# A DeltaNet and SwiGLU kernel: the first two chunks' inverse in 16x16 blocks, weights converted by an integer add, the plain FFN in whole passes

## The chip, the core and the metric

The kernel runs on one core of a Trainium2 chip. The core has five engines with a queue each: TensorE (PE) multiplies matrices into PSUM, VectorE (DVE), ScalarE (ACT) and GpSimd (POOL) work element by element, and SyncE (SP) mostly issues DMAs, as ACT's queue can too. An engine takes its instructions strictly in order and waits on semaphores for the others. The metric is device time in microseconds; less is better.

## The reference

```
k_n = k / (|k| + 1e-6)                        # B=4, H=8, S=768, D=48
for t in range(S):
    y[t] = q[t] @ state                       # per batch and head, state 48 x 48
    state += beta[t] * k_n[t] (v[t] - state^T k_n[t])^T
x = y as (B*S, H*D) = (3072, 384)
xn = x / sqrt(mean(x^2) + 1e-6) * g
out = (silu(xn @ w_gate) * (xn @ w_val)) @ w_out      # 384 -> 1536 -> 384
```

q, k, v and beta are fp32; the weights and g come as float64, which the kernel reads as pairs of 32-bit words and converts to fp32 itself.

## The kernel before

The sequence is cut into 12 chunks of 64 tokens. In a chunk the recurrence is a triangular system: with A the strictly lower part of beta * k_n k_n^T (64x64 for each of 32 pairs of batch and head), u = (1 + A)^-1 beta (v - k_n state), y = q state + mask(q k_n^T) u, and the state gains k_n^T u. `prep(c)` forms the scores and inverts (`scores`, L538), `recur(c)` makes u, y and the state (products with the state L849, with the inverse L895, with u L909 and L946), and y is transposed for the FFN (`xtr`, L1017) and scaled by g into `xf`, or `xp1` in chunk 1 (L1021).

The inverse is taken in 32x32 blocks. Scores are written to DRAM (`dkk`) and read back so that each of 128 partitions holds one 32x32 block (`at_`); DVE scales the block by beta (L654), takes a first pair of columns (L679 to L689) and then 15 steps of two instructions, a product (L701) and a sum of three (L707). The result goes through DRAM (`dx`) into `mt`, `x2bd` and `m1bd`, and PE makes the block below the diagonal in two merges (L783, L807); chunks 0 and 1 turn one block on PE as well (L759). Chunk 0 works on unscaled keys at first and divides by the norms afterwards (L607, L623 to L629).

The FFN of chunks 0 and 1 is plain (`ffn_plain`: up-projections L1084, ACT's silu L1091, DVE's product L1092, down-projections L1066); its 12 column blocks run in two halves, chunk 0's first half, chunk 1's first half, then the second halves, with the partial results in `part`. Chunks 2 to 11 use a form of fewer products (`ffn`, L1177, and `down`, L1234) on sums of weights that `factors` (L1140, L1142) and `out_factors` (L1213) make once.

The 18 weight pieces of 128 x 768 values pass three raw buffers. One takes an ACT pass (L465), two DVE passes on bits (L453, L456), one DVE pass that multiplies in the low word (L461), and a sum, by PE for the first three pieces (L478 to L483) and by DVE for the others (L486).

Nothing runs in source order. Each operation is handed to a planner (`Plan`) with an estimated duration, a priority and its dependencies; the planner simulates the engines, searches 60 orders and emits the best. `due(c, lead)` gives the time by which something of chunk c should be ready; `P.lead` puts the recurrence in front of the FFN on PE. Until a planned time of 70 us the planner fills PE's gaps with matmuls of `ident` (`fillers`, L1334), into one bank of PSUM set aside for that. The order is fixed when the kernel is built.

## Time and profile before

| what | us |
|---|---|
| runs | 714.55, 711.37, 714.91 (middle 714.55) |
| span of the profiled execution | 711.6 |
| mean granted clock of TensorE | 0.995 |

The page gives no time of the profiled execution beside its span. A group's row reads: line, engine, operation, output and inputs, shapes, count, busy us, mean ns of one, idle time before it. These rows of the page stand for the stage from chunk 2 on:

```profile
L1187 DVE TENSOR_TENSOR tmp<-tmp,bank 128x512 f32<-128x512 f32 x180 | 122.2, 685 | 88.6 <-PE bank L1177 63.0
L1177 PE MATMUL bank<-xf,w_in 128*128 128x128 f32 x1440 | 182.0, 277 | 0.0
L1177 PE MATMUL bank<-xf,more 128*128 128x128 f32 x960 | 123.9, 277 | 0.0
```

DVE idles 88.6 us in front of its additions there, mostly for PE, while these matmuls of PE wait for nothing. Matmuls are pipelined, so the mean of one (277 ns) is longer than the distance between two; prices of PE's work are taken from how long a row of many lasts.

### The profile page before, as it was taken

The numbers are of one execution on the slowest core, as the hardware profiler recorded it, in microseconds if no ns is written. First come the engines' busy times: TensorE is split into PE (matmuls) and PEld (weight loads), VectorE is DVE, ScalarE is ACT, GpSimd is POOL, SyncE is SP. The second block draws the span as 40 slices with busy tenths as digits, with TensorE's granted clock in tenths as the row PEclk, the third lists the DMA queues.
The fourth block names the chain that finished last, engine by engine and source line by source line (L and its number), as shares of the span: only waits on it lengthen the run. The fifth ranks groups of instructions, "written<-read, shape, count | busy, mean of one in ns | idle before, by whom it ended". The sixth has DMA issues, their size and how long they took to land.

```text
span 711.6 us, 23292 instructions
## 1 busy us (share of the span) xinstructions
PE 698.8 (98%) x10036; PEld 634.8 (89%) x10036; DVE 545.9 (77%) x1139; ACT 317.7 (45%) x755; POOL 135.4 (19%) x140
## 2 busy tenths in 40 slices
PE   8998998999999999999999999999999999999997
PEld 5656777777799999999999999999999998999997
DVE  4899998999648959938959948946969847976473
ACT  5435553334244445546435355345355355234441
POOL 4201203102021232223130405005040304000000
PEclk9999998999999999999999999999999999999999
DMA  7777895431351261271161262154161161040000
GB/s 138 214 156 179 221 247 137 59 62 35 51 103 25 47 111 34 55 125 34 30 114 25 46 120 51 26 99 85 17 113 17 37 99 33 13 65 2 23 1 23
DMA packets 210071, 54.67 MB, mean 77 GB/s; under 512 B 199216, under 2 KB 202288, under 8 KB 209968
## 3 DMA queue, kind: packets, MB, share of 16 engines
q1 hardware_dynamic: 205120, 52.26, 36.8%
q10 hardware_dynamic: 4848, 0.92, 0.8%
q8 instruction: 79, 1.29, 0.7%
q14 instruction: 24, 0.20, 0.1%
HBM read 40.83 MB, written 12.32 MB: 75 GB/s over the span
## 4 chain that ended last, share of the span: by engine, by line
PE 89%; DVE 6%; DMA 2%; POOL 1%; ACT 1%; issue 1%; POOLq 0%; ACTq 0%; DVEq 0%
PE bank L1177 38%; PE bank L1234 20%; PE bank L1084 9%; PE bank L1066 4%; PE bank L849 3%; PE bank L538 3%; PE bank L515 3%; PE bank L909 2%; DVE acc L707 2%; PE bank L895 2%; PE bank L1334 1%; PE bank L1017 1%; DVE acc L701 1%; PE bank L946 1%; PE bank L783 1%; PE bank L807 1%
## 5 line engine op out<-in xcount | busy, mean ns | idle before, releaser
L1187 DVE TENSOR_TENSOR tmp<-tmp,bank 128x512 f32<-128x512 f32 x180 | 122.2, 685 | 88.6 <-PE bank L1177 63.0
L1177 PE MATMUL bank<-xf,w_in 128*128 128x128 f32 x1440 | 182.0, 277 | 0.0
L1177 PEld LDWEIGHTS bank<-xf,w_in 128*128 128x128 f32 x1440 | 170.1, 192 | 2.6 <-issue 1.2
L1177 PE MATMUL bank<-xf,more 128*128 128x128 f32 x960 | 123.9, 277 | 0.0
L1177 PEld LDWEIGHTS bank<-xf,more 128*128 128x128 f32 x960 | 115.1, 192 | 1.5 <-issue 0.4
L1189 ACT COPY tmp<-bank 128x512 f32<-128x512 f32 x120 | 68.7, 584 | 65.4 <-PE bank L1177 57.2
L707 DVE TENSOR_REDUCE acc<-acc 128x30 f32<-128x90 f32 (+4 forms) x180 | 85.0, 472 | 6.2
L1193 ACT ACTIVATE tmp<-tmp 128x256 f32<-128x256 f32 x120 | 49.5, 417 | 74.5 <-DVE tmp L1187 74.0
L701 DVE TENSOR_TENSOR acc<-acc,at 128x60 f32<-128x60 f32 (+4 forms) x180 | 63.1, 351 | 2.6
L1234 PE MATMUL bank<-wo_sb,hf 128*128 128x192 f32 x360 | 63.9, 328 | 0.0
L1194 DVE TENSOR_TENSOR hf<-tmp 128x256 f32<-128x256 f32 x120 | 53.9, 463 | 12.6 <-ACT tmp L1193 11.4
L560 POOL TENSOR_TENSOR knrm<-ksum,half 128x16 f32<-128x16 f32 x12 | 36.5, 3043 | 121.3 <-DVE ksum L559 121.3
L1234 PEld LDWEIGHTS bank<-wo_sb,hf 128*128 128x128 f32 x360 | 58.1, 190 | 0.5 <-DVE hf L1194 0.2
L1334 PE MATMUL bank<-ident 128*128 128x128 f32 (+2 forms) x156 | 45.2, 437 | 1.4 <-POOL ident masks.py:199 1.4
L1334 PEld LDWEIGHTS bank<-ident 128*128 128x128 f32 x156 | 26.3, 197 | 18.9 <-issue 16.4
L654 POOL TENSOR_TENSOR at<-at,beta_b 128x1024 f32<-128x1024 f32 x8 | 18.9, 2364 | 117.0 <-DMA at<-dkk 94.7
L728 POOL COPY acc<-acc 128x128 f32<-128x128 f32 x40 | 16.5, 445 | 129.2 <-DVE acc L707 128.5
L1084 PE MATMUL bank<-xf,w_in 128*128 128x256 f32 x144 | 33.6, 384 | 0.5 <-ACT xf L1021 0.5
L1084 PE MATMUL bank<-xp,w_in 128*128 128x256 f32 x144 | 34.0, 394 | 0.0
L1066 PE MATMUL bank<-wo_sb,hf 128*128 128x384 f32 x96 | 33.6, 490 | 0.0
L1084 PEld LDWEIGHTS bank<-xp,w_in 128*128 128x128 f32 x144 | 28.1, 198 | 4.4
L1084 PEld LDWEIGHTS bank<-xf,w_in 128*128 128x128 f32 x144 | 26.7, 190 | 5.1 <-ACT xf L1021 0.7
(166 smaller groups left out, 1018.8 us busy)
## 6 DMA issues: line engine op xcount, KB each, us to landing
at<-dkk SPq DMA_DIRECT2D x23, 256.0 KB, 4.2
q<-in_q_dram SPq DMA_DIRECT2D x24, 192.0 KB, 3.8
more<-in_moe_w_val_dram SPq DMA_DIRECT2D x6, 768.0 KB, 6.1
more<-in_moe_w_gate_dram SPq DMA_DIRECT2D x6, 768.0 KB, 6.6
more<-in_moe_w_out_dram SPq DMA_DIRECT2D x6, 768.0 KB, 7.3
vt<-in_v_dram SPq DMA_DIRECT2D x24, 192.0 KB, 4.5
out_dram<-tmp SPq DMA_DIRECT2D x48, 96.0 KB, 2.2
k<-in_k_dram SPq DMA_DIRECT2D x23, 192.0 KB, 4.2
```

The costliest lines, as they stand in the source:

```text
L560: P.add("POOL", 2.95, lambda: nc.gpsimd.tensor_tensor(out=knrm[i2], in0=ksum[i2], in1=half, op=ALU.pow), pn, r=[("ksum", i2), "half"], w=[ ...
L701: nc.vector.tensor_tensor(out=acc[:, 1:3, 0:n, j + 2 : W].rearrange("p a i t -> p i a t"), in0=acc[:, old, 0:n, j : j + 2, None].to_broadc ...
L707: nc.vector.tensor_reduce(out=acc[:, new, 0:n, j + 2 : W], in_=acc[:, lo : lo + 3, 0:n, j + 2 : W].rearrange("p a i t -> p i t a"), axis=A ...
L1066: nc.tensor.matmul(po[p].t[:, 0:DM], hf[:, spot(f), 128 * p : 128 * p + 128], wo_sb[:, spot(f)], start=(f == f0), stop=(f == f1 - 1), skip ...
L1084: nc.tensor.matmul(ps.t[:, TOK * side : TOK * side + TOK], w_in[:, side, h_, 3 * t + i_, n : n + 128], x_[:, 2 * t : 2 * t + 2].rearrange( ...
L1177: nc.tensor.matmul(g.t[:, 128 * z : 128 * z + 128], fac[:, side, 128 * f : 128 * f + 128], xf[:, xs], start=(begin and z == 0), stop=False ...
L1187: P.add("DVE", V(512), lambda t=t, g=g: nc.vector.tensor_tensor(out=t, in0=t, in1=g.t, op=ALU.add), -1, r=[g], w=[tk], last=g)
L1189: P.add("ACT", A(512), lambda t=t, g=g: nc.scalar.copy(t, g.t), -1, r=[g], w=[tk], last=g)
L1193: P.add("ACT", A(256), lambda t=t: nc.scalar.activation(out=t[:, 0:256], in_=t[:, 0:256], func=ACTF.Silu), -1, w=[tk])
L1194: P.add("DVE", V(256), lambda t=t, f0=f0, p=p: nc.vector.tensor_tensor(out=hf[:, spot(f0) : spot(f0) + 2, 128 * p : 128 * p + 128], in0=t[ ...
L1234: nc.tensor.matmul(g.t[:, 0:192], a_[:, f], b_[:, f], start=(begin and f == 0), stop=(f == 5), skip_group_check=True)
L1334: nc.tensor.matmul(warm[:, 0 : 128 * w_].rearrange("p (w n) -> p w n", n=128), ident, ident[:, None, :].to_broadcast([128, w_, 128]))
```

## The change

Chunks 0 and 1 get an inverse of their own (`invert`), and nothing of it passes DRAM. From the scores, taken once per half of the heads, DVE multiplies by a coefficient per row (for chunk 0 it holds beta and the norms, `gam`, so that the keys need no scaling there; beta comes as rows that PE transposes, `betas`), folds the diagonal 32x32 blocks together, turns them by a VectorE transpose, picks the 16x16 blocks, runs 7 steps of the same kind as before on 16 columns, and turns back with four transposes. Two merges on PE (n = 0: 16 to 32, n = 1: 32 to 64), each a product with L and one with X for each half, make the full inverse; X is turned from its transpose by DVE before each merge. `recur` uses the transposed inverse directly (`mr0`) for chunks 0 and 1.

A weight piece takes two ACT passes (the high word as before, and the low word scaled by 2^-29 and written as an integer), one DVE shift and one DVE addition of 32-bit integers; PE's sums are gone. All pieces may be issued from 2 us on. The plain FFN of chunk 0 runs whole behind its recurrence, then that of chunk 1; `part` is gone. Fillers end at a planned 40 us and use free banks, no bank is set aside, and some operations carry an `urgent` priority. `due` moves from 64, 90, 160 + 51 (c - 2) to 42, 92, 143 + 51 (c - 2). Operations from chunk 2 on are the same, in a new order.

```diff
+    T0, UNTIL, V0, V1 = 42.0, 40.0, 10.0, 40.0
     def due(c, lead):
-        return (64.0 - min(lead, 64.0)) if c == 0 else (90.0 if c == 1 else 160.0 + PERIOD * (c - 2)) - lead
+        return (T0 - min(lead, T0)) if c == 0 else T0 + 50.0 + PERIOD * (c - 1) - lead
...
-            def s2(u=u):
-                nc.vector.tensor_scalar(out=u, in0=u, scalar1=3, scalar2=None, op0=ALU.logical_shift_left)
-
-            def s4(u=u, cc=cc):
-                nc.vector.tensor_scalar(
-                    out=cc.bitcast(U32), in0=u, scalar1=0xFF800000, scalar2=None, op0=ALU.bitwise_and
-                )
-
-            def s5(low=low, cc=cc, by=2.0**-52):
-                nc.vector.scalar_tensor_tensor(out=cc, in0=low, scalar=by, in1=cc, op0=ALU.mult, op1=ALU.mult)
-
...
+            def shifted(top=top):
+                nc.vector.tensor_scalar(out=top, in0=top, scalar1=3, scalar2=None, op0=ALU.logical_shift_left)
+            def added(dst=dst.bitcast(U32), top=tiled(top), rest=tiled(rest)):
+                nc.vector.tensor_tensor(out=dst, in0=top, in1=rest, op=ALU.add)
+            P.add("ACT", 0.84, lambda high=high, top=cva[a]: nc.scalar.activation(out=top, in_=high.bitcast(FP32), func=ACTF.Prelu, scale=2.0**-112, alpha=2.0**32), pr, r=[("raw", i)], w=cak)
+            P.add("ACT", 0.84, lambda low=low, rest=rest: nc.scalar.activation(out=rest, in_=low, func=ACTF.Copy, scale=2.0**-29), pr, r=[("raw", i)], w=cvk)
+            P.add("DVE", 0.57, shifted, pr, w=cak)
+            done = [("cv", n)]
+            P.add("DVE", 0.97, added, pr, r=cvk + cak, w=done)
...
+        if c == 0:
+            by_p = lambda t, p: t[:, p:16:2]
+            for p in range(2):
+                P.add("POOL", 1.6, lambda p=p: nc.gpsimd.tensor_tensor(out=by_p(knrm[0], p), in0=by_p(ksum[0], p), in1=by_p(half, p), op=ALU.pow), pn, r=[("ksum", 0), "half"], w=[("knrm", 0, p)])
+                def inv(p=p):
+                    nc.vector.tensor_scalar_add(by_p(knrm[0], p), by_p(knrm[0], p), 1e-6)
+                    nc.vector.reciprocal(by_p(krec[0], p), by_p(knrm[0], p))
+                    nc.vector.tensor_tensor(out=by_p(rb, p), in0=by_p(bt0[:, 0], p), in1=by_p(krec[0], p), op=ALU.mult)
+                    nc.vector.scalar_tensor_tensor(out=by_p(gam, p), in0=by_p(rb, p), scalar=-1.0, in1=by_p(krec[0], p), op0=ALU.mult, op1=ALU.mult)
...
+    def invert(c, pr):
+        ktk = [("kt", c % NKQ, hv) for hv in range(2)]
+        coef, ck = ((gam, [("gam", 0), ("gam", 1)]), (nbt, ["nbt"] * 2))[c]
+        L, X, XT = lx[c], xx[c], xxt[c]
+        key = lambda n, p: (n, c, p)
+        xtk = lambda p: [(key("xxt", p), i) for i in range(2)]
+        view = lambda ps, n: ps.t[:, 0 : 8 * n].rearrange("s (y n) -> s y n", n=n)
+        later = lambda lead: pr + lead
+        sp = [Group(), Group()]
+        for p in range(2):
+            def sc(p=p):
+                for u, g in units:
+                    m = kt[c][low(p), u, low(g)]
+                    nc.tensor.matmul(sp[p].t[low(g), 64 * u : 64 * u + 64], m, m)
+            P.rows = 64
+            P.add("PE", 0.53, sc, later(0.1 * p), r=ktk, w=[sp[p]], ps=sp[p], size=64)
+            P.rows = 128
+        for p in range(2):
+            P.add("DVE", 0.72, lambda p=p: nc.vector.tensor_tensor(
+                out=L[:, p], in0=view(sp[p], C), in1=coef[:, p:16:2, None].to_broadcast([128, 8, C]), op=ALU.mult,
+            ), later(1), r=[sp[p], ck[p]], w=[key("lx", p)], last=sp[p])
+            P.add("ACT", A(256), lambda p=p: nc.scalar.mul(lc[:, p], L[:, p, :, 0:W], side32[:, 0:1]), later(1), r=[key("lx", p), "sides"], w=[("lc", p)])
+            P.add("DVE", V(256), lambda p=p: nc.vector.scalar_tensor_tensor(
+                out=lc[:, p], in0=L[:, p, :, W:C], scalar=side32[:, 1:2], in1=lc[:, p], op0=ALU.mult, op1=ALU.add,
+            ), later(1), r=[key("lx", p), "sides"], w=[("lc", p)])
+        lcf = lc.rearrange("s q y n -> s (q y n)")
+        P.add("DVE", 0.66, lambda: nc.vector.transpose(out=turned, in_=lcf.rearrange("s (r j) -> s j r", j=16)), later(1.5), r=[("lc", 0), ("lc", 1)], w=["turned"])
+        def align():
+            nc.vector.tensor_scalar(out=a16, in0=turned[:, :, 0:16], scalar1=odd[:, 0:1], scalar2=None, op0=ALU.mult)
+            nc.vector.scalar_tensor_tensor(out=a16, in0=turned[:, :, 16:32], scalar=odd[:, 1:2], in1=a16, op0=ALU.mult, op1=ALU.add)
+        P.add("DVE", 0.72, align, later(2), r=["turned", "sides"], w=["a16"])
+        def start():
+            e = nc.gpsimd if c else nc.vector
+            e.memset(acc16[:, 0:4:3], 0.0)
+            e.memset(acc16[:, 0:4:3].rearrange("s a c t -> s a (c t)")[:, :, 0:256:17], 1.0)
+        P.add("POOL" if c else "DVE", 0.9 if c else 0.5, start, 0, w=["acc16"])
+        diag = a16.rearrange("s j t -> s (j t)")[:, 1 : 1 + 34 * 7 + 1 : 34]
+        def share():
+            nc.vector.tensor_tensor(out=pair16[:, :, 0:8], in0=a16[:, :, 0:16:2], in1=diag[:, None, :].to_broadcast([128, 16, 8]), op=ALU.mult)
+            nc.vector.tensor_copy(out=acc16[:, 0:4:3].rearrange("s a c t -> s a (c t)")[:, :, 1 : 1 + 34 * 7 + 1 : 34], in_=diag[:, None, :].to_broadcast([128, 2, 8]))
+            nc.vector.tensor_tensor(out=a16[:, :, 1:16:2], in0=a16[:, :, 1:16:2], in1=pair16[:, :, 0:8], op=ALU.add)
+        P.add("DVE", 0.75, share, later(3), w=["a16", "acc16"])
+        for j in range(0, 14, 2):
+            n, m = j + 2, 14 - j
+            def step(j=j, n=n, m=m):
+                old, new, lo = (3, 0, 1) if j % 4 else (0, 3, 0)
+                nc.vector.tensor_tensor(
+                    out=acc16[:, 1:3, 0:n, j + 2 : 16].rearrange("s a c t -> s c a t"),
+                    in0=acc16[:, old, 0:n, j : j + 2, None].to_broadcast([128, n, 2, m]),
+                    in1=a16[:, None, j : j + 2, j + 2 : 16].to_broadcast([128, n, 2, m]),
+                    op=ALU.mult,
+                )
+                nc.vector.tensor_reduce(
+                    out=acc16[:, new, 0:n, j + 2 : 16], in_=acc16[:, lo : lo + 3, 0:n, j + 2 : 16].rearrange("s a c t -> s c t a"), axis=AXL.X, op=ALU.add
+                )
+            P.add("DVE", 0.47 + 0.0052 * n * m, step, later(4), r=["a16"], w=["acc16"])
+        def back():
+            for side in range(2):
+                for f in range(2):
+                    t0 = 2 * side + f
+                    nc.vector.transpose(
+                        out=xc16.rearrange("s q y z t -> s t (q y z)")[:, t0:16:4],
+                        in_=acc16[:, 3 * side, :, t0:16:4].rearrange("s c k -> s k c")[:, :, None, :].to_broadcast([128, 4, 2, 16]),
+                    )
+        P.add("DVE", 1.0, back, later(8), r=["acc16"], w=["xc16"])
+        for p in range(2):
+            P.add("DVE", V(256), lambda p=p: nc.vector.tensor_tensor(
+                out=XT[:, p, :, 0:W].rearrange("s y (z t) -> s y z t", z=2), in0=xc16[:, p],
+                in1=side16[:, None, 0:2, None].to_broadcast([128, 8, 2, 16]), op=ALU.mult,
+            ), later(9), r=["xc16", "sides"], w=[(key("xxt", p), 0)])
+            def place(p=p):
+                for z in range(2):
+                    nc.scalar.mul(XT[:, p, :, W + 16 * z : W + 16 * z + 16], xc16[:, p, :, z], side16[:, 2 + z : 3 + z])
+            P.add("ACT", 0.6, place, later(9), r=["xc16", "sides"], w=[(key("xxt", p), 1)])
+        for n in range(2):
+            s = 16 << n
+            cut = lambda t, s=s: t.rearrange("s y (a two i) -> s y a two i", two=2, i=s)[:, :, :, 1]
+            each = lambda t, s=s: t.rearrange("s y (a i) -> s y a i", i=s)
+            for p in range(2):
+                P.add("DVE", 0.4 if n else 0.66, lambda p=p, e=W if n else C: nc.vector.transpose(out=X[:, p, :, 0:e], in_=XT[:, p, :, 0:e]), later(10 + 5 * n), r=xtk(p), w=[key("xx", p)])
+                P.rows = 64
+                wp, xp_ = Group(), Group()
+                def mw(p=p, wp=wp, s=s):
+                    for u, g in units:
+                        nc.tensor.matmul(
+                            wp.t[low(g), W * u : W * u + W], L[low(g), p, u],
+                            XT[low(g), p, u].rearrange("s (a two i) -> s a two i", two=2, i=s)[:, :, 1],
+                        )
+                P.add("PE", 0.7, mw, later(10 + 5 * n), r=[key("lx", p)] + xtk(p), w=[wp], ps=wp, size=64)
+                if n:
+                    P.add("ACT", A(256), lambda p=p, wp=wp: nc.scalar.mul(wx[:, p], view(wp, W), side32[:, 0:1]), later(11 + 5 * n), r=[wp, "sides"], w=[("wx", p)], last=wp)
+                else:
+                    P.add("DVE", V(256), lambda p=p, wp=wp, each=each: nc.vector.tensor_tensor(
+                        out=each(wx[:, p]), in0=each(view(wp, W)), in1=side16[:, None, 0:4:2, None].to_broadcast([128, 8, 2, 16]), op=ALU.mult,
+                    ), later(11 + 5 * n), r=[wp, "sides"], w=[("wx", p)], last=wp)
+                def mxt(p=p, xp_=xp_):
+                    for u, g in units:
+                        nc.tensor.matmul(xp_.t[low(g), W * u : W * u + W], X[low(g), p, u], wx[low(g), p, u])
+                P.add("PE", 0.7, mxt, later(12 + 5 * n), r=[key("xx", p), ("wx", p)], w=[xp_], ps=xp_, size=64)
+                P.rows = 128
+                P.add("DVE", V(256), lambda p=p, xp_=xp_, cut=cut, each=each: nc.vector.tensor_tensor(
+                    out=cut(XT[:, p]), in0=cut(XT[:, p]), in1=each(view(xp_, W)), op=ALU.add,
+                ), later(13 + 5 * n), r=[xp_], w=xtk(p), last=xp_)
...
+        kkeys, kp = kkeys_(c), [("k2p", c % NK)]
         ktk = [("kt", ikq, hv) for hv in range(2)]
-
+        if c:
+            P.add("POOL", 1.6, lambda: nc.gpsimd.tensor_tensor(
+                out=kd, in0=kd, in1=krec[i2][:, :, None].to_broadcast([128, 16, D]), op=ALU.mult,
+            ), pr if c == 1 else due(c, 125), r=[("krec", i2)], w=kkeys)
+        turn(kn, kt[ikq], ktk, kkeys + kp, pr, c == 0)
+        if c < 2:
+            invert(c, pr)
+            return
         fast = c < 4
...
+        rhs, rhsk = r_, rk
+        if c == 0:
+            P.add("POOL", 1.6, lambda: nc.gpsimd.tensor_tensor(out=vt, in0=vt, in1=rb[:, :, None].to_broadcast([128, 16, D]), op=ALU.mult), 5, r=[("gam", 0), ("gam", 1)], w=vk)
...
+            def mr0(p=p, gu=gu):
+                for bb in range(2):
+                    for y_ in range(4):
+                        for g in range(2):
+                            rows, x_, n = slice(64 * g, 64 * g + 64), 8 * bb + 4 * p + y_, 48 * (4 * bb + y_)
+                            nc.tensor.matmul(gu.t[rows, n : n + 48], xxt[c][rows, x_ % 2, x_ // 2], rhs[rows, x_])
...
-        if c == 1:
-
-            ffn_plain(0, 0, FT // 2, due(0, 0))
-            ffn_plain(1, 0, FT // 2, due(1, 0))
-            ffn_plain(0, FT // 2, FT, due(1, 0) + 23)
-            ffn_plain(1, FT // 2, FT, due(1, 0) + 46)
-            factors(0)
-            factors(1)
-            out_factors()
-        elif c > 1:
+        if c < 2:
+            ffn_plain(c, 0, FT, due(c, 0))
+            if c:
+                factors(0)
+                factors(1)
+                out_factors()
+        else:
             ffn(c, due(c, 0))
...
-        P.run([(0.0, t) for t in banks[:7]] + [(70.0, warm)], filler, 70.0)
+        P.run([(0.0, t) for t in banks], filler, UNTIL)
```

310 lines of the change are left out of this document (146 added, 164 removed).

## The prediction

> **What bounds the kernel now.** I read the page's first part, then a table of windows cut where the work changes, then the timelines of TensorE, VectorE, ScalarE and GpSimd up to 200 us.
>
> ```profile
> span 711.6 us, 23292 instructions
> PE 698.8 (98%) x10036; PEld 634.8 (89%) x10036; DVE 545.9 (77%) x1139; ACT 317.7 (45%) x755; POOL 135.4 (19%) x140
> ```
> ```profile
> 0.00:74.00 74.00, 68.73 (x858) 45.44 (x858) 59.34 (x128) 34.13 (x77) 16.54 (x19) 1.00 0.77 169
> 74.00:124.00 50.00, 47.92 (x832) 38.21 (x833) 46.66 (x81) 23.97 (x52) 8.80 (x5) 0.93 0.83 210
> 124.00:198.00 74.00, 74.00 (x655) 57.47 (x654) 63.77 (x129) 25.91 (x64) 9.43 (x12) 1.00 0.30 51
> 198.00:355.00 157.00, 156.97 (x2591) 152.40 (x2590) 121.33 (x269) 75.87 (x182) 37.64 (x37) 1.00 0.34 63
> ```
> ```profile
> 61.93 1.63 PE L895 MATMUL bank<-vt,mt 64*64 64x48 f32 x64
> 74.01 6.74 PE L1084 MATMUL bank<-xf,w_in 128*128 128x256 f32 x30 [0.46 <-ACT xf L1021]
> 197.93 1.05 PE L1177 MATMUL bank<-xf,more 128*128 128x128 f32 x8
> ```
>
> The columns of the windows are length, then busy time of PE, PEld, DVE, ACT, POOL, then granted clock, DMA share, GB/s. From 198 us on PE has no gap (156.97 of 157): there the end moves only with the amount of matmuls or with the time at which that stage starts. Before 74.01, where the first matmul of the plain FFN stands, PE's 68.73 us are mostly fillers and small products, and DVE works through the 32x32 inverse of chunk 0 and the weights. Between 74 and 198 both engines are nearly full. So the change is worth what it moves 74.01 forward, less what PE then waits before the stage at 198.
>
> **The chain of chunk 0, rebuilt.** Durations are from these rows; the order on each engine is that of the changed kernel as built.
>
> ```profile
> 8.85 0.17 DVE L559 TENSOR_SCALAR ksum<-ksum 128x16 f32<-128x16 f32 x1
> 12.27 0.25 DVE L564 RECIPROCAL krec<-knrm 128x16 f32<-128x16 f32 x1
> 12.64 1.29 DVE L607 SCALAR_TENSOR_TENSOR pt<-bank,krec 128x512 f32<-128x512 f32 x2
> 15.30 0.56 DVE L456 TENSOR_SCALAR more<-more 128x768 uint32<-128x768 uint32 x1
> 15.90 0.96 DVE L461 SCALAR_TENSOR_TENSOR more<-more 128x768 f32<-128x768 uint32 x1
> 45.77 0.96 DVE L486 TENSOR_TENSOR w_in<-more 128x768 f32<-128x768 f32 x1
> 28.26 0.22 DVE L701 TENSOR_TENSOR acc<-acc,at 128x60 f32<-128x60 f32 x1
> 28.81 0.28 DVE L701 TENSOR_TENSOR acc<-acc,at 128x112 f32<-128x112 f32 x1
> 29.50 0.32 DVE L701 TENSOR_TENSOR acc<-acc,at 128x156 f32<-128x156 f32 x1
> 41.27 0.28 DVE L707 TENSOR_REDUCE acc<-acc 128x30 f32<-128x90 f32 x1
> 79.30 0.41 DVE L1092 TENSOR_TENSOR hf<-tmp,bank 128x256 f32<-128x256 f32 x1
> ```
> ```profile
> 16.62 0.39 SPq L367 DMA_DIRECT2D more<-in_moe_w_gate_dram  x1
> 21.09 0.92 ACT L465 ACTIVATE xf<-more 128x768 f32<-128x768 f32 x1 [1.60 <-DMA more<-in_moe_w_gate_dram]
> 64.49 0.33 ACT L971 ACTIVATE yn<-bank 128x192 f32<-128x192 f32 x1 [0.58 <-PE bank L909]
> 64.72 0.19 ACT L971 ACTIVATION_READ_ACCUMULATOR yn<-bank 128x1 f32 x1
> 67.27 0.73 ACT L1004 ACTIVATE yn<-bank,rs 128x192 f32<-128x192 f32 x2
> 73.59 0.88 ACT L1021 ACTIVATE xf<-bank,g_sb 128x128 f32<-128x128 f32 x3 [0.63 <-PE bank L1017]
> 9.12 2.91 POOL L560 TENSOR_TENSOR knrm<-ksum,half 128x16 f32<-128x16 f32 x1 [3.39 <-DVE ksum L559]
> 65.87 0.65 POOL L996 TENSOR_TENSOR rs<-ms,mhalf 128x1 f32<-128x1 f32 x1 [42.86 <-DVE ms L989]
> ```
>
> Coefficients: ksum stands at 9.02 as before. The beta rows issued ahead of k on ACT's queue delay k's second half by one issue, which the copy of kt on DVE covers; uncovered they would cost under 1 us. The root now runs in two halves, each between 0.65 (one column) and 2.91 (sixteen); linearly 1.7. DVE's order holds the first weight piece's two passes before the halves' reciprocals. That piece, issued third at about 2.7, took 4.5 us from issue to use in the row at 16.62; behind k and q I take 10.3, then two ACT passes of 0.92 and an add: DVE is free at 13.1, and 8 small operations give gam at 14.9 (krec before: 12.5).
>
> Then DVE: two coefficient passes (16.3), a fold and a mask pass (17.7), first turn, alignment and first shares 2.3 (20.0). A step takes 0.55 at 60 products and 0.69 at 112 (starts 28.26, 28.81, 29.50); the seven new ones have 56, 96, 120, 128, 120, 96, 56: 2 x 0.65 + 5 x 0.70 = 4.6 with gaps (24.6), where fifteen took 13.3 (28.26 to 41.55). Turning back in four passes and two scaled copies: 26.6. No row here shows a turning pass; below, it cannot undercut the 0.22 of 60 elements, above I know of no row beyond the elementwise rate, so I take that rate (0.7 for 512). The two merges go PE, DVE or ACT, PE, DVE for each half; a pair of half-products is about 0.65, a DVE leg 0.41. Alone they would end at about 34.6, but DVE's order puts two conversions and half a third before the last additions: 38.7. PE's product with v is then at 40.0; ACT has the fifth and sixth weight pieces' passes in front of u, so u is complete at 42.1; squares (0.52 each) and scaling stand behind the passes of two more pieces on ACT, which gives 45.2 and 48.6; two transposes and two scalings: **FFN starts at 51.3**, 22.7 earlier. From the product with v to the FFN that is 12.3 us, before it was 12.1 (61.93 to 74.01).
>
> **PE's own work.** These rows price it; 64 records are 32 matmuls, since each leaves two.
>
> ```profile
> 84.14 1.16 PE L538 MATMUL bank<-kt 64*64 64x64 f32 x64
> 86.73 1.11 PE L759 MATMUL bank<-ident,wsum 32*32 32x32 f32 x64
> 92.92 0.65 PE L783 MATMUL bank<-m1bd,wsum 128*32 128x64 f32 x32
> 95.38 0.64 PE L807 MATMUL bank<-x2bd,yn 128*32 128x128 f32 x16
> 175.95 13.12 PE L1084 MATMUL bank<-xp,w_in 128*128 128x256 f32 x60
> 188.90 6.61 PE L1066 MATMUL bank<-wo_sb,hf 128*128 128x384 f32 x20
> ```
>
> After its FFN start the changed order has, more than before, one set of scores (1.1) and eight half-products of chunk 1's merges, 0.55 each if they pair like the scores, twice that if only two quadrants work at once: 0.65 taken, 5.2. It has less: 1.0 + 0.6 + 0.6. Net **+4.3** (+3.5 to +8). The plain FFN's 144 + 48 wide matmuls (an up-projection is 12 records of 13.12 / 60, so 2.6; a down-projection 4 of 6.61 / 20, so 1.3) and everything from 198 on are the same.
>
> **Chunk 1's merges on PE.** After two up-projections of 2.6 and 2.2 us of small products PE reaches the first merge of chunk 1 at 58.7. DVE can begin that inverse only after the scores just ahead of the FFN (50.6), and its queue holds conversions seven (the rest of it) and eight; with the same passes as above it is done at 64.1. Everything behind that merge on PE waits, the third up-projection first: **+5.4**. Before, this inverse was hidden under chunk 0's.
>
> **The clock.** Granted clock is the third number from the end of a window's row:
>
> ```profile
> 109.86 1.58 POOL L996 TENSOR_TENSOR rs<-ms,mhalf 128x2 f32<-128x2 f32 x1
> 108.68 1.52 PE L538 MATMUL bank<-qt,kt 64*64 64x64 f32 x64
> 112.14 1.54 PE L1017 MATMUL bank<-ident,yn 128*128 128x128 f32 x6 [1.94 <-ACT yn L1011]
> 110.00:112.00 2.00, 0.21 (x14) 0.07 (x5) 2.00 (x6) 0.53 (x2) 1.44 (x1) 0.98 1.06 243
> 112.00:114.00 2.00, 1.86 (x22) 1.52 (x23) 1.83 (x6) 1.50 (x6) 0.00 (x0) 0.50 1.05 415
> ...
> 118.00:120.00 2.00, 2.00 (x9) 1.67 (x8) 1.40 (x3) 0.01 (x1) 0.00 (x0) 0.81 0.03 6
> ```
>
> A wait of 1.94 us was followed by half clock in every window from 112 on, until 0.81 in the one from 118: about 6.8 us, 3.4 of them lost. The changed kernel's fillers end at 40 of the plan instead of 70, so PE is nearly idle from 43 to 50 and the first up-projections run at half clock; that is covered, since PE then waits for DVE anyway, and without this cover it would cost 3.4. The wait at the merges can bring a second cold stretch: none to 3.4, I take **+2**. The page "TensorE: Matmul & The Clock Gate" of the Trainium skill ("Why this matters for your kernels") warns only of idle gaps above some 3 us; this trace went to half clock after a shorter one, so its rule is the milder, and by it the 5.4 us gap alone is cold in full: 1.4 more in the sum.
>
> **The tight stretch behind it.** Up to the transposes of chunk 1's output DVE has 33.5 us in its queue (nine conversions of 1.55 make 14.0, seven factor passes of 512 elements 4.8, seven multiplies 2.9, merges with their turns 5, the rest 6.8), PE 34.8 (six up- and six down-projections 23.4, small products 11.4): even. The last transposes wait for two squares of about 0.6, an addition and the root (0.8 and 1.58) and two scalings of about 0.6 (both by the 0.33 for 192 elements), near 4.8 us after DVE's last pass, so PE stands at 98.9 until 102.8: 4.1 against 1.94 before, **+2.2**; the cold stretch there is in both. Later DVE is ahead: 73 us more (two 32x32 inverses of 13.3 + 3.3, fourteen factor passes 9.7, seventeen multiplies 7, four factor passes of 1152 elements 5.4, the rest 18) end near 171, while PE reaches the Strassen products near 190.
>
> **What costs nothing.** The second ACT pass for 18 pieces is 16.6 us; besides the places priced above it falls into ACT's idle time (24 of 50 us busy); with a full ACT it would be paid whole. The DRAM round trip of two chunks goes from the SP and ACT queues; what stood behind it were weight loads, which now start sooner but wait for a raw buffer. Whole FFN passes replace two additions by copies. The weight sums that PE made of three pieces stood among fillers, which filled the same time.
>
> **The integer add.** It is built as an instruction over 1536 16-bit halves. Its price lies between the 0.96 of a 768-word pass (45.77) and a step per half: from 0.69 for 512 (half of 1.29, with a start gap) and 0.96 for 768 each element costs 1.05 ns, so 0.96 + 0.81 = 1.77. All 768-word passes shown lie between 0.56 and 0.96, so I take 0.96. The Trainium skill ("VectorE: DVE Perf Modes", the perf-mode tier table) gives 16-bit two-tensor operations two results a cycle, fp32 one; by it the add stays at 0.96, and where no such program exists the slow end holds.
>
> **Sum** against the execution's own span: 711.6 - 22.7 + 4.3 + 5.4 + 2.0 + 2.2 = 702.8. The page gives no time around the span; it lies in the lower part of the runs (711.37 to 714.91, middle 714.55), so I add half of the 2.95 to the middle: **704**.
>
> **Rivals.** (1) The merges are covered: if DVE reaches chunk 1 about 5 us sooner, no wait and no second cold stretch stands, 711.6 - 22.7 + 4.3 + 2.2, as a run 697. For it: the chain has 4 us of conversions that wait for loads I priced late. Against: by the queue above DVE has no gap there. (2) Slower: the add takes 1.77. Its place is the DVE queue that I find without slack from 15 to 100 us; 18 x 0.81 = 14.6, all of it passed on, gives 717 in span, 718.5 as a run. It decides from 1.45 us up (8.8 us of gain over 18). A turning pass at three times the elementwise rate would act alike. Against it: every traced pass of that size. (3) The gain is eaten: PE waits for DVE all the way to the Strassen stage, which begins at 198 again; 712 to 715. For it: DVE is 93% busy from 74 to 124. Against: about 24 us of conversion passes left it (one of 0.56 and one of 0.96 for fifteen pieces, 0.56 for three), and the queue sums to 171.
>
> **How the numbers follow.** Forecast 0.47 with its own range 699 to 709; (1) 0.22; (2) 0.14; (3) 0.17. The range 692 to 716 takes in the first, the cheap end of the merges (+3.5), a chain 3 us shorter, and part of (2) and (3). About 0.5% (711 to 718) is what a measurement tells from no change: faster 0.70 (forecast, (1), a little of (3)), same 0.17, slower 0.13.
>
> **What would show it.** The first up-projection between 49 and 54; a PE wait for DVE of 3 to 8 us before the first merge of chunk 1; a window at 0.50 around it; the add at 0.95 to 1.0; seven steps in 4.4 to 4.8; the first Strassen product between 184 and 194; PE full from there. Wrong would make it: an add over 1.4, turning passes well over 0.7 per 512, weight pieces that land after 15 us, or a Strassen stage that starts after 196.

## The result, and the profile after

The changed kernel takes 706.7 us (median of six runs, 704.6 to 717.5), the kernel before beside it 714.7 (711.4 to 716.8). The ratio is 0.9894, with an interval of 0.9868 to 0.992; the ratios leave out runs with a disturbed clock, here the highest. The profiled execution has a span of 704.0 us, 7.6 less than before; the sum had given 702.8.

The page's first part and the windows of the changed kernel (columns as before: length, busy PE, PEld, which is PE's loading of weights, DVE, ACT, POOL, then clock, DMA share, GB/s):

```profile
span 704.0 us, 23411 instructions
PE 691.0 (98%) x10156; PEld 636.4 (90%) x10156; DVE 517.3 (73%) x1115; ACT 317.7 (45%) x749; POOL 141.4 (20%) x145
```
```profile
0.00:52.00 52.00, 46.62 (x718) 34.96 (x720) 36.19 (x90) 27.07 (x54) 15.88 (x21) 0.97 0.76 193
52.00:74.00 22.00, 19.69 (x307) 16.55 (x302) 18.15 (x43) 15.61 (x32) 0.00 (x0) 0.69 0.91 199
74.00:108.00 34.00, 34.00 (x530) 27.29 (x527) 26.08 (x50) 16.96 (x31) 10.17 (x7) 1.00 0.63 156
108.00:130.00 22.00, 21.37 (x278) 16.65 (x277) 20.51 (x45) 6.52 (x17) 3.48 (x6) 1.00 0.20 38
```

VectorE's work fell from 545.9 to 517.3 us, and from 74 to 108 it is busy for 26.08 of 34, while PE has no gap there. What is lost to the clock lies between 27 and 74, where it is below 1.00. PE's timeline there, and the first Strassen product (the first matmul of chunk 2's FFN, in the form of fewer products):

```profile
8.34 1.91 PE L625 MATMUL bank<-kt 64*64 64x64 f32 x64
...
27.13 2.06 PE L711 MATMUL bank<-hf 64*64 64x32 f32 x64 [2.22 <-ACT hf L697]
29.12 3.36 PE L1461 MATMUL bank<-ident 128*128 128x512 f32 x8
32.40 2.08 PE L726 MATMUL bank<-kk,hf 64*64 64x32 f32 x64
...
51.62 2.83 PE L625 MATMUL bank<-kt 64*64 64x64 f32 x64
54.39 8.10 PE L1206 MATMUL bank<-xp,w_in 128*128 128x256 f32 x24
...
66.74 3.62 PE L711 MATMUL bank<-wsum 64*64 64x32 f32 x64 [2.22 <-ACT wsum L697]
...
77.62 2.06 PE L711 MATMUL bank<-wsum 64*64 64x32 f32 x64
...
109.47 0.82 PE L1139 MATMUL bank<-ident,yn 128*128 128x128 f32 x6
...
192.46 1.05 PE L1299 MATMUL bank<-xf,more 128*128 128x128 f32 x8
```
```profile
27.00:29.00 2.00, 1.87 (x64) 1.87 (x64) 1.17 (x3) 0.66 (x3) 0.14 (x1) 1.00 0.79 271
29.00:31.00 2.00, 2.00 (x11) 0.93 (x8) 1.77 (x4) 0.00 (x0) 0.00 (x0) 0.52 0.00 1
```

The plain FFN starts at 54.39 (before 74.01, forecast 51.3). PE waits 2.22 us for chunk 1's inverse, not 5.4, then multiplies at half clock. The transposes of chunk 1's output at 109.47 wait for nothing. The first Strassen product stands at 192.46 (before 197.93); from there to the end it is 511.5 us, 2.1 less than before. Most of this is order: 192 records of q's scores (L538) stand between the FFN's start and that product, where 64 stood before, and transposes and state products of q moved with them.

VectorE's chain in chunk 0, and GpSimd beside it:

```profile
11.21 0.96 DVE L477 CUSTOM_DVE_ANT_0 w_in<-xf,tmp 128x1536 uint16<-128x1536 uint16 x1 [0.24 <-ACT tmp L480]
...
16.80 1.07 DVE L639 STREAM_TRANSPOSE at<-acc 128x512 f32<-128x512 f32 x1
...
20.86 1.29 DVE L666 TENSOR_TENSOR acc<-acc,at 128x120 f32<-128x120 f32 x1
...
25.12 1.23 DVE L682 STREAM_TRANSPOSE acc<-acc 128x128 f32<-128x128 f32 x4
```
```profile
20.54 1.47 POOL L976 TENSOR_TENSOR vt<-vt,rb 128x768 f32<-128x768 f32 x1 [8.06 <-DVE acc L666]
```

The integer add takes 0.96 us for 1536 halves, the end that the sum took. A turning pass of 512 elements read with a stride takes 1.07 instead of 0.7. One product of 120 elements takes 1.29 where its like took 0.28 (0.28 at 23.32): it ends at 22.15, just after GpSimd's pass at 22.01.

### The profile page after: what moved, and what is told of

Same layout as the page of the kernel before. It is cut to its first block, busy times and chain, and to the rows that moved or that the text cites. A ratio compares the mean times of both kernels' runs of the same rounds, so it can differ in the third digit from the quotient of the medians.

```text
span 704.0 us, 23411 instructions
## 1 busy us (share of the span) xinstructions
PE 691.0 (98%) x10156; PEld 636.4 (90%) x10156; DVE 517.3 (73%) x1115; ACT 317.7 (45%) x749; POOL 141.4 (20%) x145
## 3 DMA queue, kind: packets, MB, share of 16 engines
q8 instruction: 79, 1.29, 0.8%
## 4 chain that ended last, share of the span: by engine, by line
PE 69%; DVE 1%; issue 0%
PE bank L1299 37%; PE bank L1356 20%; PE bank L934 2%; PE bank L538 2%; PE bank L515 2%; PE bank L997 1%; PE bank L1011 1%; PE bank L1139 1%; PE bank L876 1%; PE bank L896 1%; PE bank L1068 1%; DVE hf L1316 0%; DVE tmp L1309 0%; DVE acc L828 0%; DVE yn L1099 0%
## 5 line engine op out<-in xcount | busy, mean ns | idle before, releaser
L828 DVE TENSOR_REDUCE acc<-acc 128x30 f32<-128x90 f32 (+4 forms) x150 | 70.9, 473 | 5.1
L573 POOL TENSOR_TENSOR knrm<-ksum,half 128x16 f32<-128x16 f32 x11 | 33.2, 3014 | 184.6 <-DVE ksum L559 184.6
L822 DVE TENSOR_TENSOR acc<-acc,at 128x60 f32<-128x60 f32 (+4 forms) x150 | 51.3, 342 | 1.7
L848 POOL COPY acc<-acc 128x128 f32<-128x128 f32 x40 | 20.6, 544 | 120.9 <-DVE acc L828 120.4
L1206 PE MATMUL bank<-xp,w_in 128*128 128x256 f32 x144 | 38.1, 417 | 0.0
L1213 ACT ACTIVATE tmp<-bank 128x256 f32<-128x256 f32 x24 | 9.2, 382 | 46.8 <-PE bank L1206 46.7
L1365 DVE TENSOR_TENSOR tmp<-tmp,bank 128x192 f32<-128x192 f32 x30 | 10.5, 350 | 25.1 <-PE bank L1356 25.1
```

The costliest lines, as they stand in the source:

```text
L573: P.add("POOL", 2.95, lambda: nc.gpsimd.tensor_tensor(out=knrm[i2], in0=ksum[i2], in1=half, op=ALU.pow), pn, r=[("ksum", i2), "half"], w=[ ...
L822: nc.vector.tensor_tensor(out=acc[:, 1:3, 0:n, j + 2 : W].rearrange("p a i t -> p i a t"), in0=acc[:, old, 0:n, j : j + 2, None].to_broadc ...
L828: nc.vector.tensor_reduce(out=acc[:, new, 0:n, j + 2 : W], in_=acc[:, lo : lo + 3, 0:n, j + 2 : W].rearrange("p a i t -> p i t a"), axis=A ...
L848: P.add("POOL", 1.2, lambda: spread(xt_, lambda d, t: nc.gpsimd.tensor_copy(out=d, in_=t), True), pi, w=["acc"])
L1206: nc.tensor.matmul(ps.t[:, TOK * side : TOK * side + TOK], w_in[:, side, h_, 3 * t + i_, n : n + 128], x_[:, 2 * t : 2 * t + 2].rearrange( ...
```

## The experiments

All changes are against the changed kernel, except in the last but one. Ratios are to the kernel before, run on the same chip; spans are of the profiled execution, to be held against 704.0. The order of all real work is kept but for what an edit moves; only the run with the conversion alone is planned anew, and in the one with the old conversion three of VectorE's passes stand where ScalarE's second pass stood.

**Is a cold stretch covered?** More warm-up matmuls (fillers).

```diff
-                if s < until and free and free[0][0] <= pe:
+                if s < 60.0 and free and free[0][0] <= pe:
```

> The changed kernel with more warm-up matmuls: the plan and the order of all real work are the same, but the fillers are emitted up to 60 of the plan instead of 40, which puts eight of them ahead of the output transposes of chunk 0, four around chunk 1's scores and eight ahead of chunk 1's first merge. In the profile of the changed kernel the granted clock is 0.62 and 0.52 in the two windows from 52 to 60 and 0.83, 0.50 and 0.82 from 64 to 76, with PE busy 3.91, 4.00, 1.78, 4.00 and 4.00 of them: about 1.5 + 1.9 + 0.3 + 2.0 + 0.7 = 6.4 us lost. Theory of the prediction: the first stretch is covered by the wait for chunk 1's inverse, the second (priced at 2.0) is not, so the span falls by 2 to 3.5 us, and the wait ahead of chunk 1's first merge grows from 2.2 to about 5 us, which the fillers fill. Rival 1: nothing covers either stretch, the span falls by 6 or more. Rival 2: the work behind waits for VectorE anyway, the span stays within 1 us, or grows since fillers stand in PE's queue ahead of ready work.

Ratio 0.9865 (0.9843 to 0.9886), median 704.0, span 704.2.

```profile
52.00:74.00 22.00, 20.64 (x374) 16.65 (x374) 19.10 (x46) 15.67 (x33) 0.00 (x0) 1.00 0.94 208
```
```profile
66.80 1.12 PE L711 MATMUL bank<-wsum 64*64 64x32 f32 x32 [1.36 <-ACT wsum L697]
67.85 1.57 PE L1461 MATMUL bank<-ident 128*128 128x512 f32 x6
69.35 1.12 PE L711 MATMUL bank<-wsum 64*64 64x32 f32 x32
```

The clock is 1.00 throughout, but chunk 1's merge still begins at 66.80: the first stretch was covered, as the prediction had it. Its second half waits for VectorE until 69.35, so the second stretch was half covered too: the first Strassen product came 1.4 us sooner (191.08), not 2 to 3.5, and the span did not fall in this profile, since PE lost the time again behind it (161.82 busy of the 163 us from 192, 162.83 in the changed kernel). The median of the runs is 2.7 lower, but the intervals of the two ratios overlap.

**What do half-products cost?** First the same score matmuls in another order, then the merges of chunk 1 twice.

```diff
-                for u, g in units:
+                for u, g, d in [(u, g, d) for u, g in units for d in range(2)] if not p else ():
```

> The changed kernel with one edit: the two halves' score matmuls of chunks 0 and 1 (rows L625) are issued alternately, so that all four 64 x 64 quadrants of PE's array take turns, instead of one half after the other, which uses two quadrants at a time. The matmuls are the same ones. Theory: matmuls that alternate between two quadrants run at half the rate of four; the row of L625 with 64 records falls from 1.91 us (chunk 0) to the 1.1 to 1.2 of the other scores (L538), and at half clock from 2.83 to about 2.2. Rival: the matmuls are slow for another reason (both operands come from the same tile), and the row stays at 1.9. The span: chunk 1's group stands directly ahead of the FFN, so its start moves forward by 0.5 to 1 us; if the wait for VectorE ahead of chunk 1's first merge (2.22 us) takes all that, the span stays within 0.3 us.

Ratio 0.9901 (0.9878 to 0.9924), span 705.8.

```profile
8.71 1.16 PE L625 MATMUL bank<-kt 64*64 64x64 f32 x64
27.07 3.62 PE L711 MATMUL bank<-hf 64*64 64x32 f32 x64 [2.54 <-ACT hf L697]
```

The same 64 records take 1.16 instead of 1.91: two quadrants (here one half of the rows with both halves of the columns) take 1.65 times as long as four. The span did not gain: with PE done sooner its idle time ahead of chunk 0's merge grew to 2.54, and the merge ran at half clock, 1.5 us longer.

```diff
-                    for u, g in units:
+                    for u, g in units * (2 if c == 1 else 1):
```

> The changed kernel with the sixteen matmuls of each of chunk 1's eight half-products (rows L711 and L726) issued twice into the same banks; all else is the same and in the same order. It prices the term of PE's own work. Theory: a half-product runs in two quadrants and takes 1.04 us, the upper bound of the prediction, and PE sets the end from here on: the span grows by 8.3 us (up to 9.5, since the first pair runs at half clock). With the prediction's value (0.65 each) it would grow by 5.2. Rival: PE waits for VectorE in this stretch anyway and takes most of it into those waits: under 3 us.

Ratio 1.0013 (0.9991 to 1.0035), span 715.0.

```profile
66.44 6.60 PE L711 MATMUL bank<-wsum 64*64 64x32 f32 x128 [3.72 <-ACT wsum L697]
...
202.12 1.05 PE L1299 MATMUL bank<-xf,more 128*128 128x128 f32 x8
```

The first Strassen product moves by 9.7 us, the median of the runs by 8.6. The rows L711 and L726 of chunk 1 together grow from 10.1 to 19.3 us, by 9.2, part of it at half clock (6.60 where 3.62 stood). At full clock a pair of half-products lasts 2.06, and doubling one added 1.9 (3.92). So PE sets the end there, and the eight half-products cost four times 2.06, about 8.2 us, not 5.2.

**Is VectorE's queue without slack?** The add twice, and the old conversion in the new kernel.

```diff
-                nc.vector.tensor_tensor(out=dst, in0=top, in1=rest, op=ALU.add)
+                [nc.vector.tensor_tensor(out=dst, in0=top, in1=rest, op=ALU.add) for _ in range(2)]
```

> The changed kernel with the integer add of each of the 18 weight pieces issued twice with the same operands and result: 18 x 0.96 = 17.3 us more on VectorE, nothing else moved. It tests the prediction's slower rival, which passed every us of a longer add on to the span because VectorE's queue was taken to have no slack from 15 to 100 us. That rival: the span grows by 15 to 17 us. Theory now: in the profile of the changed kernel VectorE is busy 17.2 of the 25 us from 27 to 52, 18.2 of 22 up to 74 and 26.1 of 34 up to 108, and several of its waits are for PE, so that it has slack and PE binds for part of the time: plus 5 to 11 us. If VectorE were off the path altogether: under 3 us.

Ratio 1.0069 (1.0038 to 1.0099), median 716.4: 9.7 us more for 17.3 us of VectorE (by the ratios, which take in the chips and the two longest runs, 12.5). The profiled execution is one of two among twelve that took 724; the others lie between 714.9 and 718.9.

```profile
27.00:52.00 25.00, 23.91 (x332) 21.19 (x334) 15.77 (x29) 8.08 (x14) 5.82 (x4) 0.59 0.29 92
```

Here the merges of chunk 0 ran at half clock (0.59 from 27 to 52), so that PE held up the chain. In most runs somewhat over half of the added time reaches the end; the order was made for the short add, and none was planned for the long one.

```diff
+    def old(low, rest, top):
+        nc.vector.tensor_scalar(out=top, in0=top, scalar1=3, scalar2=None, op0=ALU.logical_shift_left)
+        nc.vector.tensor_scalar(out=rest, in0=top, scalar1=0xFF800000, scalar2=None, op0=ALU.bitwise_and)
+        nc.vector.scalar_tensor_tensor(out=rest.bitcast(FP32), in0=low, scalar=2.0**-52, in1=rest.bitcast(FP32), op0=ALU.mult, op1=ALU.mult)
...
-                nc.vector.tensor_tensor(out=dst, in0=top, in1=rest, op=ALU.add)
+                nc.vector.tensor_tensor(out=dst.bitcast(FP32), in0=top.bitcast(FP32), in1=rest.bitcast(FP32), op=ALU.add)
```

> The changed kernel with the old weight conversion for all 18 pieces: on VectorE a shift, a mask, a scaled product and a float add (0.56 + 0.56 + 0.96 + 0.96 = 3.04 us) instead of a shift and the integer add (1.53), and one ScalarE pass less. The plan and the order of all else are those of the changed kernel. So VectorE has 27 us more. Theory: as with the add issued twice (17.3 us more, 9.7 us longer in the run's median), some 0.55 of it reaches the end: plus 15, near 721 as a run, which is slower than the kernel before; the new inverse needs the cheaper conversion. Rival: the pieces that lie before the FFN are hidden and the end moves by 8 or less, so that the inverse alone makes the kernel no slower than before.

Ratio 1.0218 (1.0181 to 1.0254), span 724.9 (lines are five higher in this kernel).

```profile
66.04 5.45 PE L1211 MATMUL bank<-xp,w_in 128*128 128x256 f32 x24
84.12 3.62 PE L716 MATMUL bank<-wsum 64*64 64x32 f32 x64 [10.61 <-ACT wsum L702]
```

20.9 of the 27 us reach the end, more than the theory's 15: the FFN starts 11.7 later, and PE waits 10.61 us for chunk 1's inverse. With the old conversion the new inverse, in an order planned for the new one, is slower than the kernel before.

**What made chunk 0's chain late?** GpSimd's pass moved; then the fillers ahead of the first merge made longer.

```diff
-            P.add("POOL", 1.6, lambda: nc.gpsimd.tensor_tensor(out=vt, ...
+            P.add("POOL", 1.6, lambda: None, ...
...
-            e.memset(acc16[:, 0:4:3].rearrange(...)[:, :, 0:256:17], 1.0)
+            e.memset(acc16[:, 0:4:3].rearrange(...)[:, :, 0:256:17], 1.0), c and nc.gpsimd.tensor_tensor(out=vt, ...
```

> The changed kernel with one GpSimd operation moved: the scaling of v by beta over the norm (L976, 1.47 us), which ran at 20.54 beside the inverse steps of chunk 0, is issued on GpSimd behind the clearing of chunk 1's accumulator, so that it runs at about 27. In the profile of the changed kernel the VectorE product of 120 elements at 20.86 took 1.29 us beside it, in chunk 1 0.28. Theory: the two engines got in each other's way, and 1.0 of the 3.1 us by which the FFN started later than predicted (54.39 instead of 51.3) comes from it: the product takes 0.28, the seven steps 4.5, the turned blocks are ready 1.0 us sooner. PE's wait ahead of chunk 0's first merge falls from 2.2 to 1.2; if that wait is also what halves the clock from 29 to 32.4, that stretch goes too and the FFN starts 2 to 2.5 us sooner, else 1.0. Rival: the product is slow for a reason of its own and stays at 1.29, or the slowness moves to the VectorE passes near 27: no gain.

Ratio 0.9863 (0.9833 to 0.9894), median 703.6, span 700.7.

```profile
20.98 0.28 DVE L666 TENSOR_TENSOR acc<-acc,at 128x120 f32<-128x120 f32 x1
```
```profile
26.25 2.06 PE L711 MATMUL bank<-hf 64*64 64x32 f32 x64 [1.21 <-ACT hf L697]
28.23 1.79 PE L1461 MATMUL bank<-ident 128*128 128x512 f32 x8
29.95 2.06 PE L726 MATMUL bank<-kk,hf 64*64 64x32 f32 x64
...
52.32 7.33 PE L1206 MATMUL bank<-xp,w_in 128*128 128x256 f32 x24
...
64.68 2.23 PE L711 MATMUL bank<-wsum 64*64 64x32 f32 x64 [3.01 <-ACT wsum L697]
```

The product takes 0.28, the wait ahead of the merge is 1.21, the half clock behind it is gone (fillers 1.79 instead of 3.36), and the FFN starts 2.1 us sooner. All as in the theory. The span fell by 3.3, more than that; the FFN's first groups still run partly at half clock (7.33), and PE waits 3.01 us at chunk 1's merge.

```diff
-                    filler(fillers(pe, s), free[0][1])
+                    filler(fillers(pe, s + (1.5 if 22.0 < s < 23.2 else 0.0)), free[0][1])
```

> The changed kernel with the warm-up matmuls ahead of chunk 0's first merge made 1.5 us longer (PE's fillers end at 24.9 and the merge starts at 27.13); all else is the same. Theory: the idle time of 2.2 us ahead of the merge halves the granted clock from 29.1 to 32.4 (0.54, 0.50, 0.50, 0.75 in those windows), so that the fillers between the two half-products last 3.3 us instead of 1.7 and the second half-product starts at 32.40 although its inputs were ready by 30.9: without the idle time the clock is 1.00 there, the second half-product starts at 30.9 to 31, and the FFN 1.4 us sooner. Rival: VectorE holds the chain, the clock is restored and the FFN starts where it did, within 0.4 us. Span: minus 1 to 1.5, or nothing.

Ratio 0.9905 (0.9874 to 0.9936), median 707.0, span 706.4.

```profile
26.94 2.05 PE L711 MATMUL bank<-hf 64*64 64x32 f32 x64 [0.51 <-ACT hf L697]
...
30.65 2.06 PE L726 MATMUL bank<-kk,hf 64*64 64x32 f32 x64
...
51.98 5.45 PE L1206 MATMUL bank<-xp,w_in 128*128 128x256 f32 x24
...
64.85 3.63 PE L711 MATMUL bank<-wsum 64*64 64x32 f32 x64 [5.40 <-ACT wsum L697]
```
```profile
64.00:80.00 16.00, 15.15 (x160) 13.03 (x162) 11.91 (x24) 8.56 (x17) 2.44 (x1) 0.50 0.78 198
```

The chain gained 1.75 us at L726 and the FFN starts 2.4 sooner, at 51.98, but the whole did not gain. The FFN now runs warm, PE waits 5.40 us at chunk 1's merge, and then it works at half clock until 80: some 7.5 of 15.15 us lost. The first Strassen product comes at 194.56, 2.1 later. With GpSimd's pass moved the FFN starts nearly as soon, but its cold first groups (7.33) leave a wait of 3.01, and there that product comes at 188.98.

**All together.** The two last edits (with 1.0 instead of 1.5) and the warm fillers.

> Three edits together on the changed kernel: the scaling of v moved as in the run with that alone, the warm-up matmuls ahead of chunk 0's first merge 1.0 us longer, and warm-up matmuls emitted up to 60 of the plan. Theory: no cold stretch is left, the FFN starts near 52, and the span falls by 1.0 + 1.5 + 1.4 (the last is what the first Strassen product moved with warm fillers alone) = 3.9, to about 700. Rival: the stretch from 74 to 190 is limited by VectorE and gives it back: 703 or more.

Ratio 0.9854 (0.9822 to 0.9885), median 702.2, span 700.5.

```profile
52.00:74.00 22.00, 20.68 (x342) 16.60 (x337) 20.72 (x49) 14.77 (x29) 0.00 (x0) 1.00 0.98 238
```
```profile
65.14 1.12 PE L711 MATMUL bank<-wsum 64*64 64x32 f32 x32 [1.32 <-ACT wsum L697]
```

Five of its six runs lie between 702.13 and 702.29, below every one of the changed kernel's twelve (lowest 703.75), of which six at least ran on another chip; the ratio's interval overlaps that of the changed kernel. Of the kernels in which nothing of the computation is changed it has the lowest median, but GpSimd's move alone had a span of 700.7 and a median of 703.6 on the same chip, so what the two filler edits add to it (0.2 by the span, 1.4 by the median) is not clear of noise.

Two more edits were put on it. One is the scores in four quadrants again:

> The run with three edits together (the scaling of v moved, longer warm-up ahead of chunk 0's first merge, warm-up matmuls up to 60 of the plan) and a fourth: the scores of chunks 0 and 1 issued in four quadrants, with the first warm-up 0.75 us longer still to make up for the shorter scores. Theory: at a clock of 1.00 throughout, chunk 1's scores take 1.16 instead of 1.91 us ahead of the FFN, so all that follows, chunk 1's inverse on VectorE included, moves 0.7 us forward: span 699.8, against 700.5 of the three edits. Rival: VectorE's second coefficient pass was not waiting for the second half of the scores: no change, 700.5.

Ratio 0.9864 (0.984 to 0.9888), median 704.1, span 702.8: no gain.

```profile
50.40 1.16 PE L625 MATMUL bank<-kt 64*64 64x64 f32 x64
...
64.74 1.48 PE L711 MATMUL bank<-wsum 64*64 64x32 f32 x32 [2.12 <-ACT wsum L697]
```

The scores shrank as forecast (1.91 to 1.16), but VectorE reached the merge only 0.4 us sooner. PE's idle time there grew from 1.32 to 2.12, and a stretch at 0.66 came back (64 to 68). The other edit moves one piece's shift and add behind chunk 1's inverse:

```diff
-            P.add("DVE", 0.57, shifted, pr, w=cak)
+            P.add("DVE", 0.57, shifted if n != 8 else lambda f=shifted: held.append(f), pr, w=cak)
...
-            P.add("DVE", 0.97, added, pr, r=cvk + cak, w=done)
+            P.add("DVE", 0.97, added if n != 8 else lambda f=added: held.append(f), pr, r=cvk + cak, w=done)
```

> The four edits and a fifth: the shift and the integer add of the ninth weight piece (1.5 us on VectorE, in the middle of chunk 1's fold) issued behind the scaling of chunk 1's turned blocks. Theory: chunk 1's inverse is what PE waits for ahead of that chunk's first merge (65.14 in the run with three edits, after 3.5 us of warm-up matmuls and 1.3 of idle time), so 0.8 to 1.5 us less ahead of it on VectorE moves all that follows: span 698.5 to 699. Rival: the two operations only filled VectorE's waits for ScalarE's half of the fold: no change against the four edits.

Ratio 0.9825 (0.9803 to 0.9846), median 701.1, span 699.2. In this kernel part of the computation changes: the eleventh piece's ScalarE passes into the same buffers (at 56.76 and 57.58) come before the ninth's shift (63.44), so neither piece's weights are the reference's, and ScalarE is spared a wait for the buffer. From chunk 1's scores to its merge it is 13.84 us (49.68 to 63.52) instead of 14.34 with four edits, so 0.5 of the 1.5 us lay on the path and the rest filled waits; the scores themselves came 0.7 sooner, which the edit doesn't explain. The 699.2 is no time of a usable kernel; one that keeps the wait was not tried.

**The conversion alone, in the kernel before.**

```diff
-            P.add("DVE", 0.57, s2, pr, w=cak)
-            P.add("DVE", 0.57, s4, pr, r=cak, w=cvk)
-            P.add("DVE", 0.96, s5, pr, r=[("raw", i)], w=cvk)
...
+            P.add("ACT", 0.84, lambda low=low, rest=rest: nc.scalar.activation(out=rest, in_=low, func=ACTF.Copy, scale=2.0**-29), pr, r=[("raw", i)], w=cvk)
+            P.add("DVE", 0.57, shifted, pr, w=cak)
+            P.add("DVE", 0.97, added, pr, r=cvk + cak, w=done)
```

> The kernel before with the new weight conversion alone: two ScalarE passes, a shift and the integer add for all 18 pieces; the inverse, the DRAM round trip and the order rules are those of before (the planner places the work anew). VectorE has 15 x 1.51 + 3 x 0.56 = 24 us less, ScalarE some 17 us more less six copies. Theory: with the old conversion the changed kernel was 21 us longer in span, so the cheaper conversion carries most of the gain, and here too VectorE holds the FFN's start (59.3 of 74 us busy): it starts 4 to 9 us sooner and the span falls by as much. Rival: before 74 the chain of chunk 0's 32 x 32 inverse with its DRAM round trip binds, and from 74 on PE is nearly full (47.9 of 50 us and 74.0 of 74): within 2 us. Second rival: ScalarE's longer queue delays the chain: longer by 2 or more.

Ratio 1.0089 (1.0059 to 1.0118), median 721.2, span 716.3. This is inconclusive on the conversion itself, since the planner placed all work anew and PE stood idle twice, for 3.25 us (to 69.41) and for 6.52, with nothing that the trace shows as the cause:

```profile
117.78 0.71 PE L538 MATMUL bank<-qt,kt 64*64 64x64 f32 x17 [6.52 <-issue]
```

What it does show is that the FFN did not start sooner (76.99, before 74.01); less the first idle time it would be some 73.7, an estimate, and still no gain of 4 to 9. VectorE finished the fifteen steps of chunk 0 only 1.1 us sooner (40.40 instead of 41.55). Neither half of the change was faster in the form tried here. The third part of the change, the plain FFN in whole passes, and the new `due` times and fillers were not tried alone.

**The changed kernel again.**

> The changed kernel itself, beside the others on the same chip. Its runs so far lie between 704.6 and 708.7 with clocks of 0.988 to 0.995. Expected: the same spread, a median of 705 to 707.5; the runs of the three to five edits, at a clock near 1.00, lie closer together and 3 to 6 us lower.

Ratio 0.99 (0.9863 to 0.9936), over four runs of 703.75 to 709.09; their middle, 705.7, is as expected. The span is 703.1. Part of its own scatter has a visible cause:

```profile
27.37 2.05 PE L711 MATMUL bank<-hf 64*64 64x32 f32 x64 [2.35 <-ACT hf L697]
29.36 1.79 PE L1461 MATMUL bank<-ident 128*128 128x512 f32 x8
```

After nearly the same idle time the clock stayed up here, and the FFN started at 53.42 instead of 54.39.

## Why the prediction came out, and where its steps were off

The time was right (704 forecast, 706.7 measured, span 704.0 against 702.8), and so was the main cause: the FFN starts some 20 us sooner, and about 12 of them are lost behind it. But several terms were off, with opposite signs:

| step | forecast | measured |
|---|---|---|
| FFN starts | 51.3 (-22.7) | 54.39 (-19.6) |
| PE's own extra work | +4.3 | about +8 |
| wait before chunk 1's merge | +5.4 | +2.2 |
| half clock in the FFN's first four groups | 0, covered | +2.7 (8.10 instead of 5.45), in place of waiting |
| cold clock behind that merge | +2.0 | 3.1 of PE's time, 1.4 of it at the first Strassen product |
| wait before chunk 1's transposes | +2.2 | -1.9 |
| cold stretch behind it | 0, in both | -3.4, it is gone |
| all behind the FFN's start | +13.9 | +12.0 |

The last row is a difference of the spans, each less the FFN's start: (704.0 - 54.39) - (711.6 - 74.01). The measured rows above it, from PE's work on and with 3.1 for the cold clock, add up to 10.7; where the other 1.3 lies is not shown. Measured less forecast, these rows and the start are +3.1, +3.7, -3.2, +2.7, +1.1, -4.1 and -3.4: they cancel, so that the sum came within 1.2 us is in good part luck.

Four figures of the working do not follow from their own terms: 1.1 + 5.2 less 2.2 is 4.1, not 4.3; from 98.9 to 102.8 it is 3.9, so +2.0, not +2.2; from 40.0 to 51.3 it is 11.3, not 12.3; and the seven steps make 4.6 with two of 0.55, not of 0.65. With 4.1 and 2.0 the sum is 702.4, which changes nothing that follows.

- **The start, 3.1 us late.** The working of the chain held until the inverse (gam at 13.7, forecast 14.9; turned blocks 27.1, forecast 26.6, of which the collision with GpSimd took 1.0). Two things were not in it: that collision, and the half clock behind the 2.22 us of idle time ahead of the first merge, which held the second half-product back until 32.40. The scores just ahead of the FFN took 2.83 us as well, where a set of scores was priced at 1.1. Without the idle time the start is 51.98, without the collision (and with it the idle time) 52.32. The page "SBUF — State Buffer" of the Trainium skill ("SBUF: two separate sides") says that a VectorE operation with two SBUF inputs and a GpSimd operation that reads SBUF exclude each other for a whole instruction; the row at 20.86 agrees, it ended 0.14 us after GpSimd's pass. This rule belonged in the prediction.
- **PE's work.** The step that failed is "0.65 taken, 5.2": the upper bound was the true price. In each half-product the rows and the columns in use lie in the same half of the array, so that only two quadrants take turns. The run with the scores in four quadrants shows what two cost there, though for another pair of quadrants; for the half-products it is inferred from their place in the array and their 2.06. The doubled merges show that PE pays it whole. The product of chunk 1's right side with the inverse grew for the same likely reason, from 1.1 to 2.2 us; that was not tried alone:

```profile
L1031 PE MATMUL bank<-r,wsum 64*64 64x48 f32 x64 | 2.2, 219 | 0.0
```
```profile
L895 PE MATMUL bank<-r,wsum 64*64 64x48 f32 x64 | 1.1, 221 | 0.0
```

  With four merge groups of 2.06, one set of scores of 1.1 and this 1.1, less the 2.4 that fell away, the term is 8.0.
- **The wait at chunk 1's merge.** The mechanism is right, and the run with longer fillers shows the forecast's own numbers: FFN at 51.98, wait 5.40, merge at 64.85 (forecast 51.3, 5.4, 64.1). In the changed kernel the FFN starts 2.4 us later and its first four groups take 8.10 instead of 5.45 us at half clock, while the merge comes 1.9 later (66.74): that leaves 2.2 of the 5.4.
- **The clock.** That the first cold stretch is covered was right. The second was priced as "none to 3.4", for a wait of 5.4. At the wait that came, 2.22, it took 3.1 us of PE's time (3.62 instead of 2.06, and 2.93 instead of 1.56 for the up-projection behind it), 1.4 of it at the end; at 5.40 it takes some 7.5, more than the bound. The term came near only because the wait was short.
- **The transposes.** The step "PE stands at 98.9 until 102.8" failed: PE, slower by its merges, came there only at 109.47. The chain ahead was late too, by some 7 us: its two scalings on ScalarE (L1133) ran from 108.49 to 109.61, where the prediction had them done by 102.8, so the wait went only just. The cold stretch from 112 to 119 of before, kept in the sum ("is in both"), went with the wait: 3.4 us of gain that stood nowhere.
- **VectorE without slack.** That was wrong as stated. VectorE waits for PE several times, and 17.3 us more of it cost 9.7 in most runs. But 27 us more cost 20.9, so the slower rival was sound in kind and lacked only its condition, the slow add. The first rival (697) fell: PE does wait. So did the third: the Strassen stage starts 5.5 us sooner.

## What to carry to other kernels

When a change takes work off one engine, look at how long the other one then stands idle just ahead of its next long stretch: here a wait of 5.4 us was followed by 15 us at half clock, some 7.5 of them lost, so that a start at 51.98 gave nothing, while a start at 52.32 with a wait of 3.01 gave a span of 700.7, and one at 53.02 with warm-up matmuls in that wait 700.5. Price small matmuls by the quadrants that they really use, from a row with the same pattern of operands and not from the nearest shape. And try each half of a change alone before crediting it: the cheap conversion and the short inverse were each slower than the old kernel in the one form tried, and only together faster.
